# Three small schedule edits in a fused attention and SwiGLU kernel: later memory sums for one batch, a different engine for one copy, and an even split of the last output tile

## The chip, the cores and the metric

The kernel runs on one core of one Trainium2 chip. The metric is the device time of one execution in microseconds (us). It is about 1.75 us longer than the span that the profile shows. Each comparison runs the two kernels in turn on the same chip. A run is called slow when it lies more than 1.5% above the fastest run of the same kernel.

## The reference

Eight batches of eight heads, 576 tokens and 64 columns go through attention over 32 memory slots, and the result, as 4608 tokens of 512 columns, through a gated block of width 1536.

```python
def _attn_ref(q, k, v, phi):                    # (8, 8, 576, 64), phi (8, 8, 576, 32)
    a = softmax of phi over the tokens
    k_m = np.einsum('bhsm,bhsd->bhmd', a, k)
    v_m = np.einsum('bhsm,bhsd->bhmd', a, v)
    scores = matmul(q, k_m.transpose(0, 1, 3, 2)) / sqrt(64)
    return matmul(softmax of scores over the 32 slots, v_m)

def _moe_ref(x, w_gate, w_val, w_out):          # x (4608, 512), width 1536
    g = x @ w_gate
    return (g * sigmoid(g) * (x @ w_val)) @ w_out
```

(The softmaxes are abridged.)

## The kernel before

The kernel never forms the attention output. It multiplies the memory values v_m with the weights once per batch ("U", one round per third of the width) and then applies the normalised attention A to U. One batch has 24 slots. In each slot a pair of gate matmuls and a pair of value matmuls run, and output matmuls of an earlier batch and the memory sums of the next are spread between them by a key. The program's eight PSUM tiles, which it calls banks (B0 to B7), go round in one ring: whoever asks next gets the bank that was freed longest ago.

```python
    def bank(shape, dtype, name):
        tag = free.pop(0)
        ...
    def done(*tiles):
        for t in tiles:
            free.append(held.pop(id(t))[0])

    def u_round(b, parts, evac):
        ...                                     # matmuls of U into one bank per group
        for (t, p, home, r), e in zip(banks, evac):
            if e == "a":
                if r is None:
                    nc.scalar.copy(out=t, in_=p)
                ...
            elif r is None:
                nc.vector.tensor_copy(out=t, in_=p)
            ...
            done(home)

    def u_item(b, c, evac="avav"):              # four copies: a = ScalarE, v = VectorE
        return lambda: u_round(b, (((0,), c, (0, 1)), ((1,), c, (0, 1))), evac)
```

The last output tile is computed in two halves of 256 columns, each stored over two queues. A tile of 128 tokens falls into two pieces of the output layout, here 96 and 32 rows.

```python
    def out_units_end(c, u):
        ...
                    nc.scalar.copy(out=t_o, in_=mine["p"])
                    segs = token_segments(2 * c * S + 128 * u, 128)
                    for n, (r0, m, bb, jj, pp) in enumerate(segs):
                        (nc.sync, nc.scalar)[n % 2].dma_start(
                            out=out_r[bb, jj, pp:pp + m, h * half:h * (half + 1)],
                            in_=t_o[r0:r0 + m, :],
                        )

    def out_list(b):
        tiles = range(0, 4) if b % 2 == 0 else range(4, 9)
        ...                                     # the last tile of the last batch: out_units_end
```

All loads of q, k, v and of most phi are issued by GpSimd in program order. The load of q for batch 3 writes the buffer that held q of batch 2, so GpSimd waits for the transposing load of batch 2 before it can issue that load and everything behind it: in the trace before, the transposing load landed at 66.53 us and GpSimd, which had stood for 26.2 us, issued the load at 67.12. The load of q for batch 5 waits in the same way for the transposing load of batch 3 (landed at 93.20, issued at 93.80, 22.9 us of standing).

```python
    Q_SLOT = (0, 1, 0, 0, 1, 0, 1, 0)           # the buffer of q, by batch

    load_q(2)
    load_q(3)                                   # waits for the transposing load of q(2)
    ...
    for b in range(2, B):
        ...
        if b == 2:
            load_k(3)
            load_v(3)
            load_q(4)
            load_phi(4, nc.gpsimd)
        ...
        if b == 2:
            streams += [                        # (items, first slot, last slot)
                ([lambda: load_qT(3)], 12, 12),
                (kv_items(3, lambda: (u_item(2, 2)(), run(take(2)))), 10, 14),
                ([lambda: (run(take(2)), u_three(3), run(take(3)))], 17, 18),
            ]
        ...
            if b + 3 < B:
                load_q(b + 3)                   # for b = 2: q(5), waits for the transpose of q(3)
            if b + 2 < B:
                load_k(b + 2)
                load_v(b + 2)
        ...
        if not last and b > 2:
            streams += [
                (kv_items(b + 1, lambda: (u_item(b, 2)(), run(take(2)))), 9, 14),
                ...
            ]
        spread(*streams)
```

kv_items(b) holds the memory sums of batch b (denominators, then 72 small tiled matmuls on k and v) and the transposes that follow them.

The softmax here doesn't subtract the row's maximum and nothing guards it: scores larger than these inputs give would overflow.

Of the kernel before, what the change touches and what calls it, by code (L numbers as in the profile page):

```python
# [14 lines left out]
def kernel(  # L15
# [58 lines left out]
    def bank(shape, dtype, name):  # L74
        tag = free.pop(0)
        t = ps.tile(shape, dtype, tag=tag, name=name)
        held[id(t)] = tag, t
        return t
# [5 lines that stand above are left out]
# [142 lines left out]
    def kv_sum(b, p, parts):  # L226


        w0, w1 = parts[0], parts[-1] + 1
        n = (w1 - w0) * D  # L230
        for j in range(JK):
            for i in range(NP):
                for g in range(NG):
                    nc.tensor.matmul(  # L234
                        p[g][32 * i:32 * i + 32, 0:n],
                        lhsT=phi_of(b, g, j, i),
                        rhs=kvs[b][64 * g:64 * g + 64, w0:w1, i, j * D:(j + 1) * D],
                        start=(j == 0),
                        stop=(j == JK - 1),
                        tile_position=(64 * g, 32 * i),  # L240
                    )

    def kv_denominators(b, p):

        if b in masked:
            for g in range(NG):
                for j in range(JK):
                    nc.tensor.matmul(
                        p[:, g:g + 1],
                        lhsT=masked[b][:, j, g].rearrange("p i m -> p (i m)"),  # L250
                        rhs=ones1,
                        start=(j == 0),
                        stop=(j == JK - 1),
                    )
            return
        if b in esums:
            hl = esums.pop(b)
            terms = [hl[:, t] for t in range(2)]
        else:
            terms = [ephis[b][:, j].rearrange("p i m -> p (i m)") for j in range(JK)]  # L260
        for n, x in enumerate(terms):
            nc.tensor.matmul(p, lhsT=x, rhs=ones2, start=(n == 0), stop=(n == len(terms) - 1))

    def kv_reciprocal(b, p):
        r = att.tile([128, NG], FP32, tag="rS", name="t_rS")
        nc.vector.reciprocal(out=r, in_=p)
        rSs[b] = r
# [4 lines left out]
    def k_norm(b, p):  # L272
        bk = att.tile([128, NG, 2, D], BF16, tag="bk", name="t_bk")
        for g in range(NG):
            x = p[g][:, 0:D].rearrange("p (a d) -> p a d", a=1).to_broadcast([128, 2, D])
            scaled_copy(bk[:, g], x, rSs[b][:, g:g + 1])
        bks[b] = bk

    def v_norm(b, p):
        bv = att.tile([128, NG, D], BF16, tag="bv", name="t_bv")  # L280
        for g in range(NG):
            scaled_copy(bv[:, g], p[g][:, D:2 * D], rSs[b][:, g:g + 1])
        bvs[b] = bv

    def kv_T(b, parts):
        p = bank([128, 3, 128], BF16, "p_T")
        if 0 in parts:
            kTs[b] = att.tile([128, 3, 128], BF16, tag="kT", name="t_kT")
        if 1 in parts:
            nc.tensor.transpose(p[:, 2], bvs.pop(b).rearrange("p g d -> p (g d)"), ident)  # L290
        if 0 in parts:
            bk = bks.pop(b)
            for g in range(NG):
                nc.tensor.transpose(p[:, g], bk[:, g].rearrange("p a d -> p (a d)"), ident)  # L294
        lo, hi = (0 if 0 in parts else 2), (3 if 1 in parts else 2)
        nc.vector.tensor_copy(out=kTs[b][:, lo:hi], in_=p[:, lo:hi])
        done(p)

    def kv_items(b, beside=None):


        def run_sums():
            o = 2 * D
            p = [bank([128, CH], FP32, f"p_kv{g}") for g in range(NG)]
            kv_denominators(b, p[0][:, o:o + NG])
            kv_sum(b, p, (0, 1))
            kv_reciprocal(b, p[0][:, o:o + NG])
            k_norm(b, p)
            v_norm(b, p)
            done(*p)  # L310
            if beside:
                beside()

        return [run_sums, lambda: kv_T(b, (0, 1))]
# [254 lines left out]
    def out_units(c, u, eng):  # L569

        mine = {}

        def unit(jf):
            def run():
                if jf == 0:
                    mine["p"] = bank([128, DM], FP32, "p_oo")
                nc.tensor.matmul(  # L577
                    mine["p"],
                    lhsT=hts[c, jf][:, 128 * u:128 * (u + 1)],
                    rhs=WO[jf],  # L580
                    start=(jf == 0),
                    stop=(jf == NJF - 1),
                )
                if jf == NJF - 1:
                    t_o = work.tile([128, DM], FP32, tag="to", name="t_o")
                    if eng == "a":
                        nc.scalar.copy(out=t_o, in_=mine["p"])  # L587
                    else:
                        nc.vector.tensor_copy(out=t_o, in_=mine["p"])  # L589
                    done(mine["p"])  # L590
                    for (r0, m, bb, jj, pp) in token_segments(2 * c * S + 128 * u, 128):
                        nc.sync.dma_start(
                            out=out_r[bb, jj, pp:pp + m, :], in_=t_o[r0:r0 + m, :]
                        )

            return run

        return [unit(jf) for jf in range(NJF)]
# [30 lines left out]
        return [unit(half, jf) for half in range(2) for jf in range(NJF)]  # L629

    def out_list(b):
        tiles = range(0, 4) if b % 2 == 0 else range(4, 9)
        res = []
        for n, u in enumerate(tiles):
            if b + 1 == B and u == tiles[-1]:
                res += out_units_end(b // 2, u)
            else:
                res += out_units(b // 2, u, "a" if n < 2 else "v")
        return res
# [6 lines left out]
    def u_item(b, c, evac="avav"):  # L646

        return lambda: u_round(b, (((0,), c, (0, 1)), ((1,), c, (0, 1))), evac)
# [12 lines left out]
    def run(items):  # L661
        for x in items:
            x()
# [131 lines left out]
    def take(n):  # L795
        nonlocal backlog
        n = max(0, min(n, len(backlog)))
        part, backlog = backlog[:n], backlog[n:]
        return part

    for b in range(2, B):
        last = b + 1 == B
        exp_tables()
        if b == 2:
            load_qT(2)
            phi_exp(2)
            run(take(28))
            run(kv_items(2)[:1] + take(6) + kv_items(2)[1:] + take(14))
        run(take(4))
        for g in range(NG):  # L810
            scores(b, g)
        u_values(b)
# [5 lines that stand above are left out]
        if not last:  # L818
            phi_exp(b + 1)
        nc.scalar.preload_act_table_set("silu_and_others")  # L820
        for g in range(NG):
            z_inv_v(b, g)
            norm(b, g)
        run(take(20))
        if b == 2:
            run(take(4))
            u_three(2)
        run(take(12))
        g = gv_slots(b)
        beside = 0 if last else 7  # L830
        outs = [lambda: run(take(1)) for _ in range(len(backlog) - beside)]
        streams = [(g, 0, 24), (outs, 0, 24)]
        if last:
            streams += [([u_item(b, 2)], 5, 6)]
        if b == 2:
            streams += [
                ([lambda: load_qT(3)], 12, 12),
                (kv_items(3, lambda: (u_item(2, 2)(), run(take(2)))), 10, 14),
                ([lambda: (run(take(2)), u_three(3), run(take(3)))], 17, 18),
            ]  # L840
        elif not last:
            load_qT(b + 1)
        if not last:
            if b > 2:
                phi_sum(b + 1)
            if b + 3 < B:
                load_q(b + 3)
# [4 lines that stand above are left out]
                load_phi(b + 3, nc.gpsimd)  # L852
        if not last and b > 2:
            streams += [
                (kv_items(b + 1, lambda: (u_item(b, 2)(), run(take(2)))), 9, 14),
                ([lambda: (run(take(2)), u_three(b + 1), run(take(3)))], 17, 18),
            ]
        spread(*streams)
        flush_mul()
        backlog += out_list(b)  # L860
# [29 lines left out]
```

## Time and profile before

| | before |
|---|---|
| time, median of 3 runs | 244.24 us (244.22 to 244.45) |
| time of the profiled run | 245.01 us |
| PE / VectorE (DVE) / ScalarE (ACT) busy | 96% / 71% / 66% of the span |
| start of the last matmul to the end of the span | 4.08 us |

PE is busy for 96% of the span and no edit takes out a matmul, so the time can fall only where PE stands or starts late, and after its last matmul. The prediction quotes the PE timeline around the two changed places. Here is what it doesn't quote, the end of the kernel: the view of DMA transfers over the last 4 us (destination and source, queue, number, size each, us from issue to landing).

```profile
out_dram<-t_o ACTq DMA_DIRECT2D x1, 96.0 KB, 2.0
out_dram<-t_o SPq DMA_DIRECT2D x1, 32.0 KB, 1.8
```

The slower of these two last stores lands at 241.87 us (issued at 239.87), and the span ends 1.36 us later, at 243.24.

### The profile page before, as it was taken

Reading aid. Unit: us, or ns where it says so; the run is one execution under the profiler, and the core shown is the slowest. Engines: PE = TensorE matmul, PEld = TensorE weight load, DVE = VectorE, ACT = ScalarE, POOL = GpSimd, SP = SyncE. Lnnn points to the kernel's source line nnn. Section 1 sums busy time; section 2 is a strip of 40 time slices with the busy share of each in tenths; the row PEclk is TensorE's granted clock in tenths of the full one; section 3 lists DMA queues with packets and bytes.
Section 4 is the critical chain, followed back from the end, with each engine's and each line's share of the span. In section 5 each row is a group of like instructions: output and inputs, shape, how many; then the busy total and the mean of one; then the engine's idle time right before and its main releaser. Section 6 shows DMA issues by size and latency. Waiting matters only on the chain.

```text
span 243.2 us, 6458 instructions
## 1 busy us (share of the span) xinstructions
PE 233.9 (96%) x2511; PEld 139.0 (57%) x2511; DVE 172.0 (71%) x384; ACT 160.7 (66%) x334; POOL 47.6 (20%) x77
## 2 busy tenths in 40 slices
PE   7987999999999999998999999999999999999993
PEld 2543577674545656476646665476646655567542
DVE  4347699991387788878876796879885887777310
ACT  2778789885085658965795667767895568576201
POOL 8532532000060005050505310170005000000000
PEclk9999999999999999999999999999999999999999
DMA  6999999996899965998798699199208311310143
GB/s 206 205 205 205 201 206 208 255 246 116 180 169 230 264 144 86 216 308 101 98 227 251 93 194 270 50 160 197 57 19 170 62 43 46 86 43 4 53 120 86
DMA packets 42446, 36.98 MB, mean 152 GB/s; under 512 B 15920, under 2 KB 37168, under 8 KB 42416
## 3 DMA queue, kind: packets, MB, share of 16 engines
q0 software_dynamic: 21424, 22.42, 52.8%
q1 hardware_dynamic: 20240, 13.37, 24.1%
q10 hardware_dynamic: 752, 0.79, 1.0%
q8 instruction: 19, 0.31, 0.5%
q14 instruction: 11, 0.09, 0.1%
HBM read 42.47 MB, written 9.44 MB: 213 GB/s over the span
## 4 chain that ended last, share of the span: by engine, by line
PE 81%; DMA 13%; POOL 3%; DVE 1%; issue 1%; ACT 0%; DVEq 0%; POOLq 0%
PE p_oo L577 34%; PE p_g L517 18%; PE p_v L517 18%; DMA t_kv<-in_v_dram 13%; PE p_u L474 5%; PE p_kv L234 2%; PE p_oo L609 1%; POOL t_q L108 1%; POOL t_kv L98 1%; PE p_g L403 1%; DVE t_U L498 0%; POOL t_kv L102 0%; PE p_mT L322 0%; DVE t_o L589 0%; PE p_T L294 0%
## 5 line engine op out<-in xcount | busy, mean ns | idle before, releaser
L577 PE MATMUL p_oo<-WO,t_h 128*128 128x512 bf16 x420 | 106.7, 379 | 0.0
L533 ACT ACTIVATE t_sg<-p_g 128x288 bf16<-128x288 f32 x192 | 77.0, 414 | 37.5 <-PE p_g L517 30.5
L540 DVE TENSOR_TENSOR t_h<-t_sg,p_v 128x288 bf16<-128x288 bf16 x192 | 82.1, 452 | 15.5 <-PE p_v L517 12.5
L517 PEld LDWEIGHTS <-t_U 128*128 128x128 bf16 x768 | 73.8, 98 | 32.0 <-issue 2.7
L517 PE MATMUL p_g<-t_A,t_U 128*128 128x288 bf16 x384 | 77.7, 286 | 0.0
L517 PE MATMUL p_v<-t_A,t_U 128*128 128x288 bf16 x384 | 76.9, 286 | 0.2 <-DVE t_o L589 0.2
L577 PEld LDWEIGHTS <-t_h 128*128 128x128 bf16 x420 | 39.6, 98 | 43.2 <-issue 6.4
L494 ACT CAST t_U<-p_u 128x512 bf16<-128x512 f32 x42 | 22.5, 602 | 8.8 <-PE p_u L474 8.8
L589 DVE COPY t_o<-p_oo 128x512 f32<-128x512 f32 x19 | 13.1, 688 | 17.6 <-PE p_oo L577 13.0
L498 DVE CAST t_U<-p_u 128x512 bf16<-128x512 f32 x30 | 19.0, 683 | 1.5 <-PE p_u L474 1.5
L115 POOL DMA_DIRECT2D t_q<-in_q_dram x6 | 4.8, 800 | 64.0 <-DMA t_qT<-t_q 62.5
L474 PE MATMUL p_u<-W,t_kT 64*32 64x512 bf16 (+1 forms) x416 | 15.9, 363 | 0.1
L688 PE MATMUL p_warm<-bones 128*128 128x512 bf16 (+2 forms) x43 | 12.1, 406 | 1.7 <-DVE bones L711 1.7
L587 ACT COPY t_o<-p_oo 128x512 f32<-128x512 f32 x16 | 8.9, 588 | 7.4 <-PE p_oo L577 7.3
L437 DVE TRANSPOSE_TENSOR_REDUCE t_z<-t_E 128x18 f32<-128x576 bf16 x12 | 9.3, 774 | 6.2 <-ACT t_E L414 6.2
L454 DVE TENSOR_TENSOR t_A<-t_E,t_lz 128x576 bf16<-128x576 bf16 x16 | 12.1, 757 | 0.7
L214 POOL COPY t_mark<-t_A 1x1 bf16<-1x1 bf16 x4 | 0.7, 181 | 52.1 <-DVE t_A L454 52.1
L675 ACT ACT_TABLE_LOAD x7 | 9.0, 1283 | 1.4 <-PEq L874 1.3
L414 ACT ACTIVATE t_E<-p_g 128x288 bf16<-128x288 f32 x12 | 5.0, 414 | 7.1 <-PE p_v L403 7.0
L446 DVE STREAM_TRANSPOSE t_lz<-t_z 128x576 f32<-128x576 f32 x12 | 9.3, 778 | 0.4
L496 ACT ACTIVATE t_U<-p_u,t_rS 128x512 bf16<-128x512 f32 (+1 forms) x14 | 8.1, 628 | 2.2 <-PE p_u L474 2.2
L500 DVE TENSOR_SCALAR t_U<-p_u,t_rS 128x512 bf16<-128x512 f32 (+1 forms) x14 | 8.8, 669 | 1.0 <-PE p_u L474 1.0
(70 smaller groups left out, 160.1 us busy)
## 6 DMA issues: line engine op xcount, KB each, us to landing
t_kv<-in_k_dram POOLq DMA_DIRECT2D x8, 576.0 KB, 9.7
t_kv<-in_v_dram POOLq DMA_DIRECT2D x8, 576.0 KB, 14.4
out_dram<-t_o SPq DMA_DIRECT2D x23, 192.0 KB, 2.7
t_phi<-in_phi_dram POOLq DMA_DIRECT2D x6, 576.0 KB, 16.5
t_q<-in_q_dram POOLq DMA_DIRECT2D x6, 576.0 KB, 6.7
out_dram<-t_o SPq DMA_DIRECT2D x24, 128.0 KB, 2.4
WO<-in_moe_w_out_dram POOLq DMA_DIRECT2D x3, 512.0 KB, 19.0
out_dram<-t_o SPq DMA_DIRECT2D x23, 64.0 KB, 2.3
```

Source lines behind the costliest of these rows:

```text
L437: nc.vector.tensor_reduce(out=z[:, 0], in_=es[b, g].rearrange("p r (n t) -> p (r n) t", t=32), axis=mybir.AxisListType.X, op=ALU.add, appl ...
L446: nc.vector.transpose(out=lz.rearrange("p r (n t) -> p (r n) t", t=32), in_=z[:, 1].rearrange("p (n t) -> p n t", t=1).to_broadcast([128, ...
L454: nc.vector.tensor_tensor(out=a, in0=es.pop((b, g)), in1=lzs.pop((b, g)), op=ALU.mult)
L474: nc.tensor.matmul(p[g][32 * i:32 * i + 32, o:o + n], lhsT=kTs[b][64 * g:64 * g + 64, 2, 32 * i:32 * i + 32], rhs=w_part(w, c, i, g, halve ...
L494: nc.scalar.copy(out=t, in_=p)
L498: nc.vector.tensor_copy(out=t, in_=p)
L517: nc.tensor.matmul(p[:, 0:HALF], lhsT=Us[b, c, g][:, o // 2, which, 128 * (o % 2):128 * (o % 2 + 1)], rhs=atts[b, g][:, r], start=(g == 0) ...
L533: nc.scalar.activation(out=sg, in_=gate[:, 0:HALF], func=AF.Silu)
L540: nc.vector.tensor_tensor(out=dst, in0=sg, in1=val[:, 0:HALF], op=ALU.mult)
L577: nc.tensor.matmul(mine["p"], lhsT=hts[c, jf][:, 128 * u:128 * (u + 1)], rhs=WO[jf], start=(jf == 0), stop=(jf == NJF - 1),)
L589: nc.vector.tensor_copy(out=t_o, in_=mine["p"])
L688: nc.tensor.matmul(p[:, 0:128 * a], lhsT=bones, rhs=x.to_broadcast([128, a, 128]) if a > 1 else bones, start=True, stop=True,)
```

## The change

Three edits that share no line. (a) In batches 2 to 6 the second of the four copies of U's chunk 2 goes from VectorE to ScalarE, which is meant to free VectorE where PE waits for it. (b) The sums of batch 4 come two slots later, which is meant to cover the late load of v. (c) The order of the last two output tiles is swapped, so that the very last one falls into pieces of 64 and 64 rows instead of 96 and 32.

```diff
     def out_list(b):
-        tiles = range(0, 4) if b % 2 == 0 else range(4, 9)
+        tiles = range(0, 4) if b % 2 == 0 else (4, 5, 6, 8, 7)
...
-                (kv_items(3, lambda: (u_item(2, 2)(), run(take(2)))), 10, 14),
+                (kv_items(3, lambda: (u_item(2, 2, "aava")(), run(take(2)))), 10, 14),
...
-                (kv_items(b + 1, lambda: (u_item(b, 2)(), run(take(2)))), 9, 14),
+                (
+                    kv_items(b + 1, lambda: (u_item(b, 2, "aava")(), run(take(2)))),
+                    11 if b == 3 else 9,
+                    15 if b == 3 else 14,
+                ),
```

## The prediction

> **What bounds the kernel now.** I read the page's shares first, then the chain of work that ended last in order of time, then the timeline of the places where TensorE (PE) was late.
>
> ```profile
> span 243.2 us, 6458 instructions
> PE 233.9 (96%) x2511; PEld 139.0 (57%) x2511; DVE 172.0 (71%) x384; ACT 160.7 (66%) x334; POOL 47.6 (20%) x77
> ...
> PE 81%; DMA 13%; POOL 3%; DVE 1%; issue 1%; ACT 0%; DVEq 0%; POOLq 0%
> ```
>
> PE is the bound, and no edit here removes a matmul, so all that can be won is time in which PE stands or starts late. Busy time alone doesn't show lateness, so I compared start times. In an undisturbed stretch (third fence, from 87.34 on) an output matmul takes 0.216 us from start to next start and a pair of gate or value matmuls 0.245 us. Where a row starts later than that behind the one before it, PE waited. From 54 us on, two places are much late, and both are touched by the change. About 0.09 us on either side of the small tiled matmuls recurs in every batch and stays.
>
> **Place one: the memory sums of batch 4** (timeline).
>
> ```profile
> 109.28 0.19 PE L262 MATMUL p_kv<-ones,t_ehl 128*128 128x2 bf16 x2
> 110.27 0.66 PEld L234 LDWEIGHTS <-t_ephi 64*32 64x32 bf16 x72 [0.90 <-DMA t_kv<-in_v_dram]
> 110.28 0.80 PE L234 MATMUL p_kv<-t_kv,t_ephi 64*32 64x128 bf16 x72 [0.80 <-DMA t_kv<-in_v_dram]
> ```
>
> The second denominator matmul starts at 109.31. In batches 5, 6 and 7 the sums start 0.09 us after it, so here they were due at 109.40 and came at 110.28: 0.88 us lost to the load of v. The chain shows 14.54 us of that load, but only this last 0.88 us kept PE from working; the rest ran beside matmuls.
>
> **Place two: U of chunk 2 in batch 2.** The timeline of PE alone, then of VectorE (DVE) alone:
>
> ```profile
> 85.58 0.41 PE L517 MATMUL p_g<-t_A,t_U 128*128 128x288 bf16 x2
> 85.90 0.41 PE L517 MATMUL p_v<-t_A,t_U 128*128 128x288 bf16 x2
> 86.14 0.22 PE L290 MATMUL p_T<-ident,t_bv 128*128 128x128 bf16 x1
> 86.19 0.27 PE L294 MATMUL p_T<-ident,t_bk 128*128 128x128 bf16 x2
> 86.50 0.41 PE L517 MATMUL p_g<-t_A,t_U 128*128 128x288 bf16 x2
> 87.09 0.40 PE L517 MATMUL p_v<-t_A,t_U 128*128 128x288 bf16 x2 [0.19 <-DVE t_o L589]
> 87.34 0.38 PE L577 MATMUL p_oo<-WO,t_h 128*128 128x512 bf16 x1
> 87.55 0.41 PE L517 MATMUL p_g<-t_A,t_U 128*128 128x288 bf16 x2
> ```
> ```profile
> 84.78 0.47 DVE L270 TENSOR_SCALAR t_bv<-p_kv,t_rS 128x64 bf16<-128x64 f32 x2
> 85.16 1.28 DVE L498 CAST t_U<-p_u 128x512 bf16<-128x512 f32 x2
> 86.36 0.68 DVE L589 COPY t_o<-p_oo 128x512 f32<-128x512 f32 x1
> 86.96 0.81 DVE L540 TENSOR_TENSOR t_h<-t_sg,p_v 128x288 bf16<-128x288 bf16 x2
> ```
>
> The value pair of 85.90 is 0.07 us late (85.58 + 0.245 = 85.83), the gate pair of 86.50 is 0.19 late (the transposes step by 0.056, so it was due at 86.31), the value pair of 87.09 is 0.35 late. Sum 0.61 us. Only the last carries the name of a releaser; the record hides the others behind the modelled ends of matmuls. The order of bank allocations in the program explains all three: the 85.90 matmul reuses the bank that DVE's first U copy empties (ends 85.84), the 86.50 one the bank of its second copy (86.44), the 87.09 one the bank of the output tile that DVE copies next (87.04). DVE's queue runs late here and PE waits for each of its results.
>
> [...]
>
> **The change, part by part.**
>
> (a) U three to one. In each of batches 2 to 6 the second of four copies goes from DVE to ScalarE (ACT): DVE loses 5 x 0.68 = 3.4 us, ACT gains 5 x 0.60 = 3.0 us. Neither is the bound (71 and 66%), so only PE's late starts count. Batch 2, walked with the measured steps: ACT copied at 84.26 and 84.74, steps near 0.5 us; with three copies the second ends near 85.4 and the third near 85.95. DVE has one copy, from 85.16 to 85.84, and the output tile's copy then runs from 85.76 to 86.44. The value pair due at 85.83 finds its bank free since 85.4; the gate pair, now due at 86.24, since 85.95; the second value pair, due at 86.49, since 86.44. All of 0.61 us goes but perhaps 0.01: **0.60 us**. What ACT pays: its next Silu starts about 0.5 us later (85.26 to 85.8) and ends at 86.2; the first bank that needs it is asked for near 86.95. In batches 3 to 6 nothing late follows these copies (0.05 us, 0.18 in batch 5, before them, waiting for DVE's scaled copies, which come earlier in DVE's order): **0 us** there. The Silus lag there by the same half microsecond, and each bank they free is asked for some 0.45 us after its release.
>
> (b) Sums of batch 4 two slots later. By the order of the two programs, eight gate/value matmuls and one output matmul move ahead of the sums: 8 x 0.1225 + 0.216 = 1.20 us. Without (a) the sums would be due at 109.40 + 1.20 = 110.60, behind the landing. With (a) PE gets there 0.60 earlier, at 110.00. The load also comes sooner: the output tile freed by (a) is stored ahead of the transposing load of q for batch 3 on the same queue (stores from 87.07, transpose at 88.29), and GpSimd's loads of k and v wait behind that transpose. If that carries through, v permits a start at 110.28 - 0.60 = 109.68 and 0.3 us is spare; if the load doesn't move at all, 0.28 us of wait is left. Gain **0.88 us**, or 0.6 at worst. The transposes behind the sums follow two slots later too; their copy still has over 1 us before the next U round uses it. No matmul is added.
>
> (c) The last tile. The end of the timeline:
>
> ```profile
> 238.82 1.36 SPq L622 DMA_DIRECT2D out_dram<-t_o x2
> 239.47 0.37 ACT L618 COPY t_o<-p_oo 128x256 f32<-128x256 f32 x1 [0.89 <-PE p_oo L609]
> 239.87 0.38 ACTq L622 DMA_DIRECT2D out_dram<-t_o  x1
> ```
>
> Two stores start at 239.87; the one of 96 rows lands after 2.0 us, that of 32 rows after 1.8. With 64 and 64 the slower should land between these: **0.05 us**, with 0.1 as its limit, since bytes and engines are the same.
>
> Sum: 0.60 + 0.88 + 0.05 = 1.53 us; 244.24 - 1.53 = **242.7 us**.
>
> **Rivals.** First, *the load's wait stays in part*: v's DMA takes 14.5 us beside three other loads and stores, so starting sooner need not land it sooner. For it: the DMA share stays near full from 94 to 111 us. Against: two slots alone cover the wait to within 0.3. It would make 243.0. Second, *ACT takes DVE's place*: three copies in a row delay Silus, so banks and products come late and the next U round, which starts three slots later, waits. For it: each slot needs a Silu of 0.41 on ACT, and its lag is worked off only at some 0.1 us a slot. Against: ACT still had gaps of 0.25 to 0.65 us between Silus here, and the walk left 0.4 us to the banks. If each of five batches lost 0.1 to 0.2 us, gain (a) would vanish: about 243.4. Third, *the bank wait only moves*: with DVE's lag removed, the first value pair behind the sums still waits for the scaled copies. That is counted above as staying. Fourth, *the tail gains nothing*, or loses as much, because the longer store on SyncE's queue follows a backlog: 242.75.
>
> **Range and chances.** The two main gains rest on start times in one trace and on separate mechanisms. Both full with a better tail: 242.5. The remaining load wait: 243.0. One of the two lost: 243.3 to 243.6. The before runs spread by 0.23 us. So 242.3 to 243.4 for 8 in 10. A change by 2% is 4.9 us, three times all there is to win, and nothing here could cost that.
>
> **What would show it.** Right: the sums of batch 4 start 0.09 us behind their denominators, with no wait for v by PE; around 86 us PE's gate and value pairs follow at 0.245 us; no wait of PE for DVE's t_o; the transposing load of q for batch 3 is issued about 0.6 us sooner; ACT's busy time is up by 3.0 and DVE's down by 3.4 us; the last store lands 1.9 us after its issue. Wrong: PE waits for ACT's U or Silu after the sums, the wait for v persists, or a late start appears in batches 3 to 6 that wasn't there.

The copies of 0.68 and 0.60 us in part (a) are the trace's own (683 ns on VectorE, 602 on ScalarE, the means in the view of the trace before by lines and forms), and the 0.05 of part (c) is the author's estimate from the two landings of 2.0 and 1.8 us.

## The result, and the profile after

| | before | after |
|---|---|---|
| time, median of 4 runs | 244.25 us (244.22 to 244.45) | 244.0 us (243.76 to 244.44) |
| ratio, 95% interval | | 0.999 (0.9973 to 1.0007) |
| time of the profiled run | 245.01 us | 243.76 us |
| start of the last matmul to the end of the span | 4.08 us | 4.28 us |

Here and below a ratio is the mean time of one kernel's fast runs over that of the other's of the same rounds, so it is not quite the ratio of the medians beside it. The two kernels can't be told apart in this comparison; the prediction, 242.7 with a range of 242.3 to 243.4, was 1.3 us too low.

The page of the changed kernel, its span, busy shares and chain of waits:

```profile
span 242.0 us, 6458 instructions
...
PE 233.7 (97%) x2511; PEld 139.1 (57%) x2511; DVE 170.1 (70%) x379; ACT 162.5 (67%) x339; POOL 47.6 (20%) x77
...
PE 88%; DMA 7%; POOL 2%; issue 0%; ACT 0%; POOLq 0%
```

Five instructions moved from VectorE to ScalarE. The two *profiled* spans differ by 1.2 us while the two medians differ by 0.25: the first warning that the pair of traces shows something that the changes alone don't make.

The timeline of PE around U of chunk 2 in batch 2 (start, duration, engine, line, operation), then of VectorE, then of ScalarE:

```profile
85.74 0.41 PE L517 MATMUL p_g<-t_A,t_U 128*128 128x288 bf16 x2
85.99 0.41 PE L517 MATMUL p_v<-t_A,t_U 128*128 128x288 bf16 x2
86.23 0.22 PE L290 MATMUL p_T<-ident,t_bv 128*128 128x128 bf16 x1
86.29 0.28 PE L294 MATMUL p_T<-ident,t_bk 128*128 128x128 bf16 x2
86.40 0.41 PE L517 MATMUL p_g<-t_A,t_U 128*128 128x288 bf16 x2
86.65 0.40 PE L517 MATMUL p_v<-t_A,t_U 128*128 128x288 bf16 x2
86.89 0.38 PE L577 MATMUL p_oo<-WO,t_h 128*128 128x512 bf16 x1
```
```profile
85.32 0.68 DVE L498 CAST t_U<-p_u 128x512 bf16<-128x512 f32 x1
85.92 0.68 DVE L589 COPY t_o<-p_oo 128x512 f32<-128x512 f32 x1
```
```profile
84.42 1.56 ACT L494 CAST t_U<-p_u 128x512 bf16<-128x512 f32 x3 [0.99 <-PE p_u L474]
85.85 0.74 ACT L533 ACTIVATE t_sg<-p_g 128x288 bf16<-128x288 f32 x2
```

Every pair now follows the one before it by 0.25 us, and the gate pair behind the transposes by 0.11, two transpose steps: the three late starts that the prediction added up to 0.61 us are gone. ScalarE makes its three copies in one row of 1.56 us, VectorE's one copy is done at 86.00, and the Silus follow without holding PE up.

The timeline of PE at the sums of batch 4:

```profile
110.03 0.19 PE L262 MATMUL p_kv<-ones,t_ehl 128*128 128x2 bf16 x2
110.16 0.80 PE L234 MATMUL p_kv<-t_kv,t_ephi 64*32 64x128 bf16 x72
```

No wait stands here. But v landed only at 110.03, and the sums were due at 110.16: 0.13 us were to spare, not the 0.3 predicted. In this trace the landing was at 110.03 and in the one before at 110.23, so the load hardly came sooner. In their old place, 1.20 us earlier by the prediction's count, the sums would have been due at 108.96, ahead of the landing; the section on all runs comes back to this.

The last 4 us: the DMA transfers, then the two issuing queues, each in its own view.

```profile
out_dram<-t_o SPq DMA_DIRECT2D x1, 64.0 KB, 1.9
out_dram<-t_o ACTq DMA_DIRECT2D x1, 64.0 KB, 2.2
```
```profile
238.42 0.47 SPq L622 DMA_DIRECT2D out_dram<-t_o  x1
```
```profile
238.42 0.50 ACTq L622 DMA_DIRECT2D out_dram<-t_o  x1
```

Two stores of 64 rows hold their queues for 0.47 and 0.50 us, where the uneven pair held them for 0.32 and 0.38, and the slower one lands 2.21 us after its issue instead of 2.00. The tail (from the start of the last matmul to the end of the span) has become longer.

So (a) looks as predicted, (b) shows no wait and (c) has the wrong sign. Read naively, the traces even confirm the sum of the prediction: 245.01 fell to 243.76. The medians don't. The experiments ask which of the two is the kernel.

### The profile page after: what moved, and what is told of

The parts are those of the page before. It is cut to its first block, busy times and chain, and to the rows that moved or that the text cites. A ratio compares the mean times of both kernels' runs of the same rounds, so it can differ in the third digit from the quotient of the medians.

```text
span 242.0 us, 6458 instructions
## 1 busy us (share of the span) xinstructions
PE 233.7 (97%) x2511; PEld 139.1 (57%) x2511; DVE 170.1 (70%) x379; ACT 162.5 (67%) x339; POOL 47.6 (20%) x77
## 4 chain that ended last, share of the span: by engine, by line
PE 88%; DMA 7%; POOL 2%; issue 0%; ACT 0%; POOLq 0%
PE p_oo L577 38%; PE p_g L517 20%; PE p_v L517 20%; DMA t_kv<-in_v_dram 7%; PE p_u L474 5%; PE p_kv L234 2%; PE p_oo L609 1%; POOL t_q L108 1%; PE p_g L403 1%; POOL t_kv L98 1%; POOL t_kv L102 0%; PE p_mT L322 0%; PE p_T L294 0%; PE p_kv L262 0%; PE p_T L290 0%
## 5 line engine op out<-in xcount | busy, mean ns | idle before, releaser
L540 DVE TENSOR_TENSOR t_h<-t_sg,p_v 128x288 bf16<-128x288 bf16 x192 | 83.1, 452 | 16.6 <-PE p_v L517 13.4
L494 ACT CAST t_U<-p_u 128x512 bf16<-128x512 f32 x47 | 24.9, 602 | 8.1 <-PE p_u L474 8.1
L589 DVE COPY t_o<-p_oo 128x512 f32<-128x512 f32 x19 | 13.1, 688 | 17.4 <-PE p_oo L577 11.8
L498 DVE CAST t_U<-p_u 128x512 bf16<-128x512 f32 x25 | 16.0, 683 | 1.5 <-PE p_u L474 1.5
L688 PE MATMUL p_warm<-bones 128*128 128x512 bf16 (+2 forms) x43 | 12.7, 422 | 1.7 <-DVE bones L711 1.7
```

The costliest lines, as they stand in the source:

```text
L540: nc.vector.tensor_tensor(out=dst, in0=sg, in1=val[:, 0:HALF], op=ALU.mult)
L589: nc.vector.tensor_copy(out=t_o, in_=mine["p"])
L688: nc.tensor.matmul(p[:, 0:128 * a], lhsT=bones, rhs=x.to_broadcast([128, a, 128]) if a > 1 else bones, start=True, stop=True,)
```

## The experiments

Theory A says: the 0.88 us before the sums of batch 4 was an accident of the one execution that was profiled; the typical run of the kernel before doesn't have it, so (b) wins nothing in the median. Rival B says: the wait is there in every run, (b) removes it, and something else (the tail, ScalarE's later Silus) gives most of it back. Rival C says: each part costs what it wins. All twelve kernels gave correct results; each was timed in 5 rounds beside the kernel before on the same chip. That kernel had medians of 244.75 (e1 to e4), 244.50 (e5 to e8) and 244.38 (e9 to e12), 11 runs each.

### e1: the kernel before, unchanged, once more

No edit.

> The kernel before, unchanged, for a second trace. Theory 1 (the profile of before was of an unlucky execution: its own run took 245.01 us against a median of 244.25, and most of the 0.88 us wait for v belongs to that execution): time within 0.1 us of before; if the profiled run is near the median, the memory sums of batch 4 start less than 0.3 us late. Theory 2 (the wait for v is there in every run, and the gain is eaten elsewhere): the sums start 0.8 to 1.0 us late again.

Measured: 244.41 us (244.22 to 244.87), ratio 0.998 (0.9948 to 1.0011), beside runs of the same kernel. The profiled run took 244.87. The timeline of PE at the sums of batch 3, then of batch 4:

```profile
82.83 0.37 PE L262 MATMUL p_kv<-ones,t_ephi 128*128 128x2 bf16 x9
83.89 0.80 PE L234 MATMUL p_kv<-t_kv,t_ephi 64*32 64x128 bf16 x72 [0.69 <-DMA t_kv<-in_v_dram]
```
```profile
109.97 0.19 PE L262 MATMUL p_kv<-ones,t_ehl 128*128 128x2 bf16 x2
110.09 0.63 PE L234 MATMUL p_kv<-t_kv,t_ephi 64*32 64x128 bf16 x51
```

The same program, one more execution: the sums of batch 4 come on time, and those of batch 3 are late. (The window that was asked for ends at 110.5 us, so the last line counts only 51 of the 72 matmuls; the cut lines of e2 and e7 below are of the same kind.) Where nothing is late the sums of batch 3 begin 0.30 us behind the first denominator (e7 below), so 83.13 was due, and 0.76 us were lost. Nobody would have thought of delaying batch 4 after reading this trace. The three late starts around 86 us are here as well. This speaks for theory A and against B, which wants the wait for batch 4 in every run. It is not a clean test: the late batch 3 also put off the time at which the sums of batch 4 were due. Without its 0.76 us that would have been 109.33, and v landed at 109.66. The cleaner evidence is e3, and the arithmetic of the times: 245.01 less 0.88 and 244.87 less 0.76 both give 244.1, about the fastest runs of this kernel (244.04 to 244.22).

### e2: only (a)

```diff
-  u_item(2, 2)()          and  u_item(b, 2)()
+  u_item(2, 2, "aava")()  and  u_item(b, 2, "aava")()
```

> Three to one copies alone. Both theories: the three late starts around 86 us are gone in the trace, 0.6 us there. Theory 1: the time falls by 0.5 to 0.6 us, to about 243.7. Theory 2: the gain is lost again behind the wait for v if the load does not come sooner (time down by under 0.2 us), as the sums of batch 4 would come earlier and wait longer.

Measured: 243.75 us (243.58 to 246.3), ratio 0.9976 (0.9935 to 1.0017). The median is 0.66 us under e1's. The profiled run was by chance the longest of the six, 246.3 us, and shows why: PE at the sums of batch 3, and later at the scores of batch 6.

```profile
83.05 0.37 PE L262 MATMUL p_kv<-ones,t_ephi 128*128 128x2 bf16 x9
84.58 0.42 PE L234 MATMUL p_kv<-t_kv,t_ephi 64*32 64x128 bf16 x32 [1.16 <-DMA t_kv<-in_v_dram]
```
```profile
177.21 0.29 PE L403 MATMUL p_g<-t_qT,t_kT 64*32 64x288 bf16 x1 [1.41 <-DMA t_qT<-t_q]
```

Two loads were late in this one execution, by 1.23 us (84.58 against 83.35) and by 1.47 us; together they are 2.7 us, and this run is 2.55 us above the median. The late starts around 86 us are gone nevertheless. So in this case a waiting PE tells little about the next execution when what it waits for is a load: the sums of batch 3 were 0, 0.76 and 1.23 us late in the traces before, e1 and e2.

### e3: only (b)

```diff
-  ..., 9, 14)
+  ..., 11 if b == 3 else 9, 15 if b == 3 else 14)
```

> Sums of batch 4 two slots later, alone. Theory 1: time falls by under 0.2 us. Theory 2: it falls by 0.6 us or more.

Measured: 244.65 us (244.38 to 247.11), ratio 1.0005 (0.9965 to 1.0046): nothing won. In its trace v of batch 4 landed at 108.55 us, and without the move the sums would have been due at 109.54: they would not have waited anyway. Three small late starts appeared in and behind the U round of batch 3 (0.16 us inside U's matmuls, at 111.73, then 0.04 at 113.59 and 0.19 at 114.19). Together they cost what the whole stretch shows: from the first output matmul to the sums of batch 5 PE took 81.46 us, against 81.08 in e7, where no load is late and nothing was moved. So the move alone not only wins nothing, it costs 0.38 us in this trace; that VectorE is behind at that place is the likely reason, not a tested one. Theory A holds; B, which needs 0.88 us won here, does not.

### e4: only (c)

```diff
-  range(4, 9)
+  (4, 5, 6, 8, 7)
```

> Tile order with two last stores of 64 rows, alone. My prediction: 0.05 us faster. New reading of the trace after (issue of a 64-row store 0.47 us against 0.32 for 96 or 32 rows; last landing 2.21 us after its issue against 2.00): 0.2 us slower, about 244.45.

Measured: 244.93 us (244.25 to 245.86), ratio 1.0006 (0.9974 to 1.0039). Times can't resolve a tenth here; the trace can: from the start of the last matmul to the end of the span 4.27 us, as in the changed kernel and against 4.13 and 4.11 in e1 and e2. Its profiled run had late sums of batch 3 again (0.45 us).

### e5: the changed kernel, unchanged, once more

No edit to the changed kernel.

> The changed kernel, unchanged, beside runs of before on one chip. Theory (of the predicted 1.53 us, 0.60 from the copies is real in every run, the 0.88 of the wait for v was the accident of one execution, and the tail costs 0.15 us where 0.05 was to be won): trace without the three late starts around 86 us; end of the span 4.27 us after the last matmul's start against 4.1 for before; median 0.3 to 0.6 us under before, with runs over a microsecond longer than the fastest where a load is late. Rival (the prediction was right and the first comparison unlucky): 1.3 to 1.6 us under before.

Measured: 244.32 us (243.91 to 245.2), ratio 0.9993 (0.9957 to 1.0028); 0.18 us under the median of before. Its profiled run, 243.91 us, had no late start at 86 us and a tail of 4.28 us. The run that was profiled was the fastest of six; the spread of 1.3 us shows that the changed kernel hasn't lost the accidents.

### e6: (a) and (b) without (c)

The diffs of e2 and e3 together.

> The change without the tail's part: copies three to one and the sums of batch 4 later. Theory: 0.15 us under the changed kernel in the fastest runs, about 243.6 against 243.75; end of the span 4.1 us after the last matmul's start. Rival (the tail is neutral): no difference in that distance.

Measured: 244.16 us (243.67 to 244.87), ratio 0.9977 (0.9944 to 1.0009), 0.16 us under e5's median, with a tail of 4.13 us. The two intervals overlap widely, so the times alone would not show it, but the sign and the size agree with the traces' 0.15 us.

### e7: the cure for the load instead of the later sums

k and v of batches 3 and 4 are loaded ahead of q of batches 3 and 5, which is needed later (the same loads are taken out of their old places, which the cut diff leaves out). A one-element copy on GpSimd, which reads the transposed q, keeps the start of each group of loads about where it was: v of batch 3 was issued near 68.0 us and v of batch 4 near 96.0 (the landings below less the 11.8 and 9.5 us to landing), against 68.64 and 95.69 before.

```diff
-    load_q(3)                                   # ahead of the loop
...
         if b == 2:
+            after_qT(2)
             load_k(3)
             load_v(3)
+            load_q(3)
...
-                ([lambda: load_qT(3)], 12, 12),
+                ([lambda: (load_qT(3), after_qT(3), load_k(4), load_v(4), load_q(5),
+                           load_phi(5, nc.gpsimd))], 12, 12),
```

> Before, with k and v of batches 3 and 4 loaded ahead of q of batches 3 and 5 (same bytes, same start of each group of loads; the first of each group still starts when the transposed q has landed). Theory (late v in either batch makes the spread of the runs): v lands 4 us or more before it is due in both batches, no wait of PE for v in the trace, fastest runs still at 244.1 to 244.2, nearly all runs under 244.5. Rival (DMA is simply short, the wait moves to q): PE waits for the transposed q of batch 3, 4 or 5, and the spread stays at 1 us or more.

Measured: 244.19 us (244.06 to 244.43), ratio 0.9978 (0.9948 to 1.0008). The loads of k and v of batch 3 in the view of DMA issues from 67 to 70 us, before and then with k and v first (size each, us to landing):

```profile
t_kv<-in_k_dram POOLq DMA_DIRECT2D x1, 576.0 KB, 9.6
t_kv<-in_v_dram POOLq DMA_DIRECT2D x1, 576.0 KB, 14.3
```
```profile
t_kv<-in_k_dram POOLq DMA_DIRECT2D x1, 576.0 KB, 8.5
t_kv<-in_v_dram POOLq DMA_DIRECT2D x1, 576.0 KB, 11.8
```

and PE at the sums of batch 3 in e7 (the lines' numbers are shifted by five):

```profile
83.31 0.37 PE L267 MATMUL p_kv<-ones,t_ephi 128*128 128x2 bf16 x9
83.61 0.61 PE L239 MATMUL p_kv<-t_kv,t_ephi 64*32 64x128 bf16 x49
```

v of batch 3 now lands at 79.75 us, 3.9 us ahead of its use, and v of batch 4 at 105.53, 4.3 us ahead. From batch 2 on PE waits for v nowhere. The median fell by 0.31 us against the kernel before, but the fastest run is no faster (244.06 against 244.04 there). What went is the upper end: the kernel before reached 246.57 us, this one 244.43. The kernel before had 11 runs and e7 six, so a part of this could be chance. It is what theory A says of such waits: they are the spread and a part of the median, not a fixed cost.

### e8: e7 with (a), and with the queues of the last two stores exchanged

```diff
-  (nc.sync, nc.scalar)[n % 2].dma_start(
+  (nc.scalar, nc.sync)[n % 2].dma_start(
```

> Copies three to one, k and v first as in the run before, sums where they were, and the last two stores with queues swapped (96 rows on SyncE's queue, 32 on ScalarE's). Theory: 0.6 us from the copies and no late v: median 243.5, fastest 243.4; the swap takes up to 0.1 us off the distance from the last matmul to the end (4.0 to 4.1 us). Rival: without the sums moved, v of batch 4 is still late in some runs.

Measured: 243.55 us (243.51 to 243.82), ratio 0.9953 (0.9923 to 0.9983). Against e7 that is 0.64 us, the size predicted for (a), now without late loads in either kernel and with runs that don't overlap (e8's slowest 243.82, e7's fastest 244.06). The exchange also settles what made one store slower than the other in the kernel before: with 96 rows on SyncE's queue and 32 on ScalarE's, the landings stay at 1.84 us for SyncE and 2.00 for ScalarE.

```profile
out_dram<-t_o SPq DMA_DIRECT2D x1, 96.0 KB, 1.8
out_dram<-t_o ACTq DMA_DIRECT2D x1, 32.0 KB, 2.0
```

Between these two pieces it is the queue, not the number of rows.

### e9: e8 without the exchange

> On the base whose loads are not late (k and v first), copies three to one in batches 2 to 6, the rest as before. Theory: 243.55 us, spread under 0.4; so the swapped queues of the last stores in e8_best gave nothing (in its trace the store on ScalarE's queue lands after 2.00 us with 32 rows as it did with 96). If the swap was worth its 0.1: 243.65.

Measured: 243.53 us (243.37 to 243.62, 5 runs), ratio 0.9953 (0.9919 to 0.9986). As far as two chips can be compared, the exchange was worth nothing; the tails are 4.07 us with it and 4.10 without. This is the fastest kernel, 0.85 us under the kernel before and with a spread of 0.25 us.

### e10: e9 with (b)

The diff of e3 on top.

> The base of e9 and the sums of batch 4 two slots later. Theory: with v in time the move is worth 0.0 us (within 0.1 of e9). Rival (the move is good for something besides the wait for v): 0.1 us or more under e9.

Measured: 243.88 us (243.54 to 244.06), ratio 0.9967 (0.9933 to 1.0001), 0.35 us above e9 in both the median and the mean. Where v is never late the move certainly wins nothing. Whether it costs 0.35 us stays open: in the one profiled run PE needs no longer from the moved sums to the next batch than in e9; that run began its output matmuls 0.30 us later, ahead of any changed line, and had one late start of 0.13 us in batch 5, which traces of several kernels have and others don't.

### e11: e9 with (c)

The diff of e4 on top.

> The base of e9 and the changed tile order with two last stores of 64 rows. Theory: 0.15 us over e9, and 4.27 us from the last matmul's start to the end of the span in the trace. As predicted on record: 0.05 under e9.

Measured: 243.64 us (243.54 to 243.88, 5 runs), ratio 0.996 (0.9927 to 0.9994); 0.11 us above e9 in the median, 0.19 in the mean. The tail is 4.27 us against e9's 4.10. With the late loads out of the way, times and traces agree that (c) costs between 0.1 and 0.2 us.

### e12: e9 with (a) in batch 2 alone

```diff
-  u_item(b, 2, "aava")()      # batches 3 to 6
+  u_item(b, 2)()
```

> The base of e9 but three to one in batch 2 alone. As predicted on record (batches 3 to 6 are worth nothing): within 0.05 us of e9. Rival (a late start of 0.13 us in batch 5 that some traces without three to one show and others don't is cured by it): 0.1 us over e9.

Measured: 243.68 us (243.44 to 243.98), ratio 0.9959 (0.9928 to 0.999), 0.15 us above e9 in the median, with overlapping runs; the two traces show the same starts. It is inconclusive: that the copies of batches 3 to 6 are worth 0 agrees with the trace, but 0.1 us can't be excluded.

### All profiled runs side by side

How late the sums of batches 3 and 4 started, in every trace, beside the time of that very run. It is the table from which theory A is read.

| trace | loads as in | run, us | batch 3 late | batch 4 late |
|---|---|---|---|---|
| before | before | 245.01 | 0 | 0.88 |
| e1 | before | 244.87 | 0.76 | 0 |
| e2 (a) | before | 246.30 | 1.23 | 0 |
| e3 (b) | before | 244.70 | 0 | 0 |
| e4 (c) | before | 244.99 | 0.45 | 0 |
| after | before | 243.76 | 0 | 0 |
| e5, after again | before | 243.91 | 0 | 0 |
| e6 (a), (b) | before | 243.86 | 0 | 0 |
| e7 to e12 | k and v first | 243.37 to 244.43 | 0 | 0 |

Of the four traces with the sums of batch 4 in their old place and the loads in their old order (before, e1, e2, e4), one has the wait that the change was made for and three have one that it doesn't touch. v of batch 3 landed between 14.26 and 15.79 us after its issue in the eight traces with the old loads, and PE needed it 14.6 to 15.1 us after.

The zeros of the last column hide one thing. In "after" and e5 v of batch 4 landed at 110.03 us, and in the old place the sums would have been due at 108.96 and 108.98. An estimate, if the load had landed at the same time: without (b) PE would have waited about 1.1 us in both. In e6, the third trace with (a) and (b), v landed at 108.11, in time for either place. So v of batch 4 is not late in one execution alone: by the old place it comes late in three of eight traces, and in two of them (b) covered it. Theory A holds for the medians, because the typical run of the kernel before has no such wait to lose. That (b) never does anything doesn't follow, and what it is worth in the median beside (a), with the old loads, no two runs show. Rival C fits (c), which costs more than it was to win, and (b) without (a), but not (a).

## Why the prediction was wrong, point by point

**(a), predicted 0.60 us: right.** The walk through the banks held. The late starts are gone in every trace with "aava"; from the first output matmul to the sums of batch 5 PE takes 80.48 us in the trace after against 81.08 before (its 0.88 us taken off), and e7 against e8 gives 0.64 us in the times. No wait for a late Silu came up, so the second rival fell. Busy times moved less than predicted, by +1.8 us on ScalarE and -1.9 on VectorE instead of +3.0 and -3.4; the page counts the time in which the engine is busy at all, and neighbours overlap (three copies of 0.60 took 1.56 us), while the prediction added up durations. Added up over all instructions of the two traces, durations rose by 3.2 us on ScalarE and fell by 3.3 on VectorE, about as predicted; the overlap grew by 1.4 us on ScalarE (12.7 to 14.1) and shrank by 1.4 on VectorE (13.4 to 12.0).

**(b), "Gain 0.88 us, or 0.6 at worst": this is the step that failed.** The working of the 0.88 from the timeline is right for that execution. It failed in what it was taken from: the wait belonged to a run of 245.01 us, and it was subtracted from a median of 244.24, in which it mostly isn't. 245.01 - 0.88 = 244.13, which is about the fastest runs of the kernel before (244.04 to 244.22): that is what an execution without the wait costs *before* the change. The difference of 0.77 us between the profiled run and the median would have shown it. The sub-step "if that carries through, v permits a start at 109.68" failed as well: the transposing load of q for batch 3 was issued 0.54 us sooner (87.75 against 88.29), as predicted, but landed at 93.68 against 93.20, so v of batch 4 was issued 0.48 us later and landed only 0.20 sooner. The first rival, that starting sooner need not land sooner, was true of the transposing load; no wait of PE came of it.

**What stays in place.** The move treats batch 4 only. The load of v for batch 3 is as close to its use as before, which is the likely reason why the changed kernel still spreads (243.91 to 245.2 in e5). Why the same load takes up to 1.5 us longer in one execution than in another isn't settled by these runs.

**(c), "0.05 us, with 0.1 as its limit": wrong sign.** The slower landing was not between 1.8 and 2.0 us but 2.21, and the tail grew by 0.16 us: 4.27 us as the mean of four traces with the even split (4.27 to 4.28), 4.11 of the nine with the old pieces and queues (4.08 to 4.14). The step took the difference between the two old stores for one of rows. e8 shows that it is one of the queue, 0.16 us more on ScalarE's. With the even split that store, the last to land (the span ends 1.36 us after it in both traces, before and after), held its queue 0.12 us longer and landed 0.16 us later (2.20 to 2.21 us after its issue in four traces, against 2.00 to 2.07); that the one makes the other is likely, but not shown. Why a store of 64 rows holds a queue longer than one of 96 isn't shown either; that it does could have been read in the trace before, where the first of two full-width stores on SyncE's queue mostly took 0.47 to 0.49 us to issue with 64 rows and 0.32 to 0.33 with 96 or 32.

**The sum.** With the terms as measured, the change is worth -0.60 (a) + 0 (b beside (a), against a run without the accident: e9, without (b), takes the same 80.48 us up to the sums of batch 5 within 0.01) + 0.16 (c) = -0.44 us. The medians show -0.25 and, in e5, -0.18. What is missing stays open; it is of the size of the jitter: late loads in some runs of either kernel, and a first output matmul that starts between 54.55 and 55.03 us in the traces, ahead of any changed line. The range was too narrow for the same reason as the step: it took the spread of three runs, 0.23 us, for that of the kernel, which reached 2.8 us (244.1 to 246.9). One end of it doesn't follow from its own terms: both gains with a tail of 0.1 give 242.66, not 242.5.

## What to carry to other kernels

Before pricing a wait seen in a trace, compare the time of the profiled execution with the median; if it is longer by about the wait, the wait may not be in the typical run, and a wait for a load needs a second trace before it is worth an edit. Here a load that was sometimes late was better cured by ordering the queue by need (e7 to e9: v lands 2.7 to 5.3 us ahead of its use, and six runs or five spread by 0.25 to 0.37 us, where 11 of the kernel before spread by over 2) than by moving its consumer by the amount that one trace shows. Read issue time and landing time by shape and by queue, where the trace already has them, before reshaping the last stores.
